# The sums of one weight pair on VectorE instead of GpSimd, traced one tile sooner: linear attention and a gated feed-forward layer

## The chip, the cores and the metric

The kernel runs on one core of one Trainium2 chip. The metric is device microseconds of one execution; of several runs the median counts. Beside the times there is one execution taken with the hardware profiler, whose trace is read below. In the text PE is TensorE, DVE is VectorE, ACT is ScalarE, POOL is GpSimd, SP is SyncE, as the profile writes them.

## The reference

Eight batches of eight heads, 576 positions, head size 64: linear attention (softmax of q over the head size, softmax of k over the positions, then q times the product of k and v). Its result, 4608 rows of 512, goes through a gated layer of width 1536.

```python
q_s = exp(q - max(q, -1)); q_s /= sum(q_s, -1) + 1e-9
k_s = exp(k - max(k, 2));  k_s /= sum(k_s, 2) + 1e-9
kv = einsum('bhsd,bhse->bhde', k_s, v)
x = einsum('bhsd,bhde->bhse', q_s, kv)      # then rows of B*S by H*D = 4608 x 512
out = ((x @ w_a) * (x @ w_b)) @ w_out       # 512 -> 1536 -> 512
```

The weights arrive as the bits of 64-bit floats and are turned into 32-bit floats on the chip.

## The kernel before

The 4608 rows are worked on in nine chunks of 512. The width 1536 is cut into twelve tiles f of 128, and two tiles make a pair i, six pairs in all. Each matmul of the large products is done three times, with a rounded high part and a remainder of each operand (`split`: ScalarE makes the high part at line 79, VectorE the remainder at line 82).

*The first chunk* is also the start of the kernel, in which everything is loaded and converted. For the tiles f = 2 to 11 one loop runs. In a round it loads weights two tiles ahead (`load_f`), converts the next tile's (`convert_ab`, `convert_wo`: ScalarE at line 103, VectorE at 107 and 113, GpSimd at 110), does a piece of the attention of the second and third chunk (`tasks`), multiplies the chunk with the tile's two weight halves (`gate_part`, line 510) into the banks k0 and k1, empties k0 by ScalarE (`gate_half`, `ga`, line 517), multiplies k1 onto it by VectorE (`gate_end`, line 521) and adds the product of the tile before with `w_out` to the output banks (`project_first`, line 545, `po`). The converted weights are stored to memory as `dy` (plain) and `dw` (split).

*From the second chunk on*, the product of a pair is done as a two by two block product with seven multiplications instead of eight (`product`, line 535: banks kx, ky, ka, kp). Four of the seven weight operands are sums of blocks: S1, S3, S2, S4. In the second chunk they are made pair by pair by `sums(i)`: four loads of `dy` into tiles `ws_y` (line 217, SyncE's queue), and four additions of 128x512 (line 225), on GpSimd, S1 first, then S3, S2 and S4, where S2 and S4 each read an earlier sum. `split_w` makes high part and remainder of each, and `put_w` stores it (line 204) for the later chunks, which load it again (`get_w`, line 208). The operands of the chunk itself (T1 to T4 and three blocks) come from `x_operands`: VectorE's differences at lines 484, 489 and 494, and splits into `xo`.

`sums(0)` is called in the last round, f = 11, and `sums(i + 1)` in the second chunk's pair i. So GpSimd makes the sums of the first pair (i = 0) and of the second one after the other. The first pair's four loads wait for room in the eight tiles of the name `wy`, which the conversion uses too.

Between the chunks stands a piece of attention for the third chunk: TensorE turns a maximum (pm, line 261), VectorE reduces it (line 263) and spreads it on a diagonal (line 265), TensorE adds that up (pmx, line 271), VectorE subtracts it (276), ScalarE takes the exponential (279), TensorE multiplies keys and values (pk, line 312), and VectorE scales the product (320 to 323, 81, 82). In the second chunk's pair i, VectorE adds ky to the copy u of kx (line 1098, made by ScalarE at 1097), ka to that (1100), then kp (1111), and so on.

*What sets the order.* The order of TensorE in the first chunk and that of the first tiles on the other engines is written out by hand (`in_order`). Elsewhere a scheduler places each engine's instructions when the program is built, from the order in which they are traced and from an estimate of the times; `issue_after(x)` keeps what is traced under it behind x. On the chip each engine then takes its instructions in that fixed order and waits on semaphores. The bank k0 holds the gates of the last tile before it holds kx of the second chunk's first pair, so kx waits for line 517.

Of the kernel before, what the change touches and what calls it, by code (L numbers as in the profile page):

```python
# [29 lines left out]
def linear_attention_then_gated_ffn(  # L30
# [18 lines left out]
    nc = tc.nc  # L49
# [4 lines left out]
    NF = 2 * NI  # L54
# [72 lines left out]
    def load_f(f):  # L127

        i, r = divmod(f, 2)
        for half in range(2):  # L130
            raw = sb.tile([P, DM], I64, name="raw", tag="xo", bufs=11)
            ins = nc.sync.dma_start(out=raw, in_=w_ab[i, r, half])
            raws[f, half] = raw
        raw = const.tile([P, DM], I64, name=f"wo{f}_raw", tag=f"wo{f}")
        with tc.issue_after(ins.ins):
            nc.sync.dma_start(out=raw, in_=w_out[f])
        raws[f, "o"] = raw
        return ins
# [20 lines left out]
    def convert_wo(f):  # L159
        y, parts = float_parts(raws.pop((f, "o")), wo_home(f))  # L160
        for part in parts:
            part()
        keep_wo(f, y)

    def split_wo(f):
        if f < 4:
            wo[f] = const.tile([P, 2, DM], F32R, name=f"wo{f}_w", tag=f"wo{f}")
        split(wo[f][:, 0], wo[f][:, 1], wo_first[f])
# [14 lines left out]
    def convert_ab(f, half):  # L183

        keep_ab(f, half, *whole_ab(f, half, to_float(raws.pop((f, half)))))
# [22 lines left out]
        nc.sync.dma_start(out=w.bitcast(F32), in_=dw[i, op].bitcast(F32))  # L208
        return w

    def sums(i):

        a = {}
        for r in range(2):
            for h in range(2):
                a[r, h] = sb.tile([P, DM], F32, name="ws_y", tag="wy", bufs=8)
                nc.sync.dma_start(out=a[r, h], in_=dy[i, r, h])
        sub, add = ALU.subtract, ALU.add
        for o, x, y, op in (
            ((1, 1), (1, 0), (1, 1), add),  # L220
            ((1, 0), (0, 0), (1, 0), sub),
            ((0, 0), (1, 1), (0, 0), sub),
            ((0, 1), (0, 1), (0, 0), sub),
        ):
            nc.gpsimd.tensor_tensor(out=a[o], in0=a[x], in1=a[y], op=op)
        return {S1: a[1, 1], S3: a[1, 0], S2: a[0, 0], S4: a[0, 1]}


# [247 lines left out]
    def x_operands(xf, which, box):  # L476

        b11, b12 = xf[:, 0:2, 0:H], xf[:, 0:2, H:T]
        b21, b22 = xf[:, 2:4, 0:H], xf[:, 2:4, H:T]
        for op in which:  # L480
            if op == T2:
                t1, t2 = t_tile(), t_tile()
                nc.vector.tensor_tensor(out=t1, in0=b12, in1=b11, op=ALU.subtract)
                nc.vector.tensor_tensor(out=t2, in0=b22, in1=t1, op=ALU.subtract)
                box["t1"], box["t2"] = t1, t2
                src = t2
            elif op == T3:
                src = t_tile()
                nc.vector.tensor_tensor(out=src, in0=b22, in1=b12, op=ALU.subtract)
            elif op == T1:  # L490
                src = box["t1"]
            elif op == T4:
                src = box["t2"]
                nc.vector.tensor_tensor(out=src, in0=b21, in1=src, op=ALU.subtract)
            else:
                src = {B11: b11, B21: b21, B22: b22}[op]
            o = xo_tile([P, 2, 2, H])
            split(o[:, 0], o[:, 1], src)
            box[op] = o


    def gate_banks(tags):
        return [ps.tile([P, T], F32, name=f"pt{n}", tag=tag) for n, tag in enumerate(tags)]

    def gate_part(f, x, n, pairs, pt):

        for g in pairs:
            w = blocks[f, g // 2][:, n, :, g % 2]
            for i, (wp, xp) in enumerate(((0, 0), (0, 1), (1, 0))):
                nc.tensor.matmul(  # L510
                    pt, w[:, wp], x[g][:, xp],
                    start=(g == 0 and i == 0), stop=(g == NP - 1 and i == 2),
                )

    def gate_half(f, pt):
        ga = sb.tile([P, T], F32, name="ga", tag=f"gh{f % 2}", bufs=1)
        nc.scalar.copy(out=ga, in_=pt)  # L517
        return ga

    def gate_end(ga, pt):  # L520
        return nc.vector.tensor_tensor(out=ga, in0=pt, in1=ga, op=ALU.mult)
# [21 lines left out]
    def project_first(f, g, po):  # L543
        for t in range(TT):
            nc.tensor.matmul(  # L545
                po[t], g[:, t * P:(t + 1) * P], wo_first[f],
                start=(f == 0), stop=(f == NF - 1),
            )
# [257 lines left out]
    at = {}  # L806
# [179 lines left out]
    sy = {}  # L986
# [21 lines left out]
    for f in range(2, NF):  # L1008
        if 1 < f - 1 < NF - 3:
            tasks[f - 1][0]()  # L1010
        if f + 2 < NF:
            load_f(f + 2)

        with tc.issue_after(at["end", f - 2].ins):
            convert_wo(f)
            if f + 1 < NF:
                convert_ab(f + 1, 0)
                convert_ab(f + 1, 1)


        n = f - 3
        if n < 0:
            copies = ()
        else:
            copies = tasks[n][2]()
        if n + 1 < NF - 3:
            with tc.issue_after(startup[0]), tc.issue_after(at["end", max(f - 2, 1)].ins):
                tasks[n + 1][1]()
        if f == NF - 1:
            with tc.issue_after(at["end", f - 1].ins):  # L1030
                split_wo(0)
                split_wo(1)
            sy[0] = sums(0)
            x_operands(xfs[1], early + late, xo)
        if f > 2:
            pts = gate_banks(("k0", "k1"))
            for h in range(2):
                gate_part(f, x0, h, range(NP), pts[h])
                if h == 0:
                    with ExitStack() as pinned:  # L1040
                        for copy in copies or ():
                            pinned.enter_context(tc.issue_after(copy.ins))
                        at["ga", f] = gate_half(f, pts[0])
            at["end", f] = gate_end(at["ga", f], pts[1])
        if n >= 0:
            tasks[n][3]()
        project_first(*pending, po)
        pending = (f, at["ga", f])
    in_order((E.PE,), by_hand, len(traced))
# [15 lines left out]
    for c in range(1, NCH):  # L1065
# [3 lines left out]
        x, xo = xo, {}  # L1069
        for i in range(NI):  # L1070
# [19 lines left out]
            if c == 1:  # L1090
                if i + 1 < NI:
                    sy[i + 1] = sums(i + 1)
                    split_wo(2 * i + 2)
                    split_wo(2 * i + 3)
# [8 lines left out]
            end = c == NCH - 1 and i == NI - 1  # L1103
# [78 lines left out]
```

## Time and profile before

| | |
|---|---|
| median of 3 runs | 975.72 us (975.56 to 975.88) |
| the profiled execution | 974.85 us |
| its span in the trace | 972.8 us |
| granted clock of TensorE, mean | 0.995 |
| TensorE busy | 942.0 us, 97% of the span |
| VectorE busy | 632.7 us, 65% |
| ScalarE busy | 393.0 us, 40% |
| GpSimd busy | 108.1 us, 11% |

Busy time of TensorE is modelled at its end, so 97% is no measure of how well it is used; it says that it hardly waits. The first 186 us hold the first chunk and the beginning of the second; the shares of the table are means over stages that differ, so the waits and the order of time are read below, and not the shares.

### The profile page before, as it was taken

What the parts mean: (1) busy time and instruction counts of PE and PEld (TensorE: products, weight loads), DVE (VectorE), ACT (ScalarE), POOL (GpSimd) and SP (SyncE); (2) the same over time, 40 slices, a digit from 0 to 9 for tenths busy, and PEclk for the clock granted to TensorE, in tenths of its full rate; (3) what the DMA queues carried; (4) which work ended last, traced back from release to release, by engine and by line L of the source; (5) the groups of instructions that cost most, each with busy time, mean ns of one, the idle gap of its engine ahead of it and who ended that gap; (6) DMA issues with size and microseconds to landing.
All of it is one profiled execution on the core that took longest, in us unless ns stands there. A gap on an engine that the chain in (4) does not pass through costs nothing.

```text
span 972.8 us, 16975 instructions
## 1 busy us (share of the span) xinstructions
PE 942.0 (97%) x6159; PEld 843.8 (87%) x6159; DVE 632.7 (65%) x1245; ACT 393.0 (40%) x1085; POOL 108.1 (11%) x92
## 2 busy tenths in 40 slices
PE   4989998999999999999999999999999999999998
PEld 3656765899999999999998999999999999999997
DVE  7986878987686747665665657565766446653433
ACT  7777754553372416332443235223623263221101
POOL 1544443522000000000000000000000000000000
PEclk9999998999999999999999999999999999999999
DMA  9999585989999968897788779877998687767761
GB/s 353 412 382 361 207 292 190 405 290 340 311 346 279 366 237 264 308 375 254 263 307 330 283 250 344 305 282 259 338 295 281 233 315 249 293 224 276 254 209 58
DMA packets 97586, 282.60 MB, mean 290 GB/s; under 512 B 11680, under 2 KB 12256, under 8 KB 97504
## 3 DMA queue, kind: packets, MB, share of 16 engines
q1 hardware_dynamic: 97504, 281.52, 81.1%
q8 instruction: 49, 0.80, 0.3%
q14 instruction: 33, 0.27, 0.1%
HBM read 241.40 MB, written 37.98 MB: 287 GB/s over the span
## 4 chain that ended last, share of the span: by engine, by line
PE 82%; DVE 7%; DMA 4%; issue 3%; ACT 2%; SPq 1%; POOL 1%; DVEq 0%; POOLq 0%; ACTq 0%
PE po L556 27%; PE kp L535 14%; PE ka L535 13%; PE kx L535 13%; PE ky L535 7%; PE pk L312 3%; PE px L466 2%; DMA ws<-dw 1%; DVE wy L113 1%; DMA dy<-wy 1%; PE po L545 1%; PE pt L510 1%; POOL wr L110 1%; DMA raw<-in_w_ab 1%; ACT wy L103 1%
## 5 line engine op out<-in xcount | busy, mean ns | idle before, releaser
L556 PE MATMUL po<-wo_w,gh 128*128 128x512 f32 x768 | 230.8, 396 | 0.0
L535 PE MATMUL kx<-xo,ws 128*128 128x256 f32 x1152 | 163.9, 284 | 3.2 <-ACT ga L517 3.2
L556 PEld LDWEIGHTS po<-wo_w,gh 128*128 128x128 f32 x768 | 138.7, 189 | 26.3 <-ACT gh L79 0.3
L535 PE MATMUL ka<-xo,ws 128*128 128x256 f32 x1152 | 161.3, 283 | 0.0
L535 PE MATMUL kp<-xo,ws 128*128 128x256 f32 x1152 | 156.7, 283 | 1.4 <-DVE u L1098 1.4
L535 PEld LDWEIGHTS kx<-xo,ws 128*128 128x128 f32 x1152 | 150.2, 189 | 6.1 <-ACT ga L517 3.6
L535 PEld LDWEIGHTS ka<-xo,ws 128*128 128x128 f32 x1152 | 149.9, 189 | 3.9 <-issue 0.5
L535 PEld LDWEIGHTS kp<-xo,ws 128*128 128x128 f32 x1152 | 146.8, 189 | 3.9 <-issue 1.6
L556 PE MATMUL po<-wo_w,gl 128*128 128x512 f32 x384 | 140.2, 396 | 0.0
L79 ACT CAST gh<-cc 128x512 fp32r<-128x512 f32 x96 | 57.6, 621 | 131.3 <-DVE cc L1122 124.5
L1121 DVE TENSOR_TENSOR cc<-kp,u 128x512 f32<-128x512 f32 x48 | 33.2, 691 | 103.7 <-PE kp L535 103.7
L1112 ACT COPY cc<-kx 128x256 f32<-128x256 f32 x48 | 17.9, 372 | 185.8 <-PE kx L535 185.8
L556 PEld LDWEIGHTS po<-wo_w,gl 128*128 128x128 f32 x384 | 71.6, 188 | 16.3 <-DVE gl L82 0.4
L380 ACT ACTIVATE qt<-qt,st 128x64 f32<-128x64 f32 x224 | 74.9, 338 | 25.2 <-DVE st L377 18.3
L1111 DVE TENSOR_TENSOR cc<-kp,u 128x512 f32<-128x512 f32 x48 | 32.9, 686 | 71.7 <-PE kp L535 71.5
L535 PE MATMUL ky<-xo,ws 128*128 128x256 f32 x576 | 77.8, 284 | 1.1 <-DMA ws<-dw 1.1
L535 PEld LDWEIGHTS ky<-xo,ws 128*128 128x128 f32 x576 | 72.1, 189 | 1.9 <-DVE xf L658 1.2
L510 PE MATMUL pt<-xo,ws 128*128 128x512 f32 x288 | 71.8, 406 | 1.1 <-DVE ws L925 1.1
L82 DVE TENSOR_TENSOR gl<-cc,gh 128x512 fp32r<-128x512 f32 x96 | 66.5, 700 | 8.1 <-ACT gh L79 8.1
L510 PEld LDWEIGHTS pt<-xo,ws 128*128 128x128 f32 x288 | 54.7, 193 | 14.3 <-DVE ws L925 1.5
L244 POOL PARTITION_ALL_REDUCE mx<-m x20 | 14.4, 722 | 460.8 <-DVE m L255 429.6
L1097 ACT COPY u<-kx 128x512 f32<-128x512 f32 x48 | 28.0, 583 | 81.1 <-PE kx L535 81.0
(144 smaller groups left out, 1202.6 us busy)
## 6 DMA issues: line engine op xcount, KB each, us to landing
ws<-dw SPq DMA_DIRECT2D x312, 512.0 KB, 5.3
dw<-ws SPq DMA_DIRECT2D x42, 512.0 KB, 6.8
mr<-dq SPq DMA_DIRECT2D x112, 128.0 KB, 4.2
raw<-in_w_ab SPq DMA_DIRECT2D x24, 512.0 KB, 7.7
out<-ot SPq DMA_DIRECT2D x36, 256.0 KB, 4.4
vt<-in_v SPq DMA_DIRECT2D x28, 325.0 KB, 7.7
qt<-in_q SPq DMA_DIRECT2D x32, 256.0 KB, 5.6
kt<-in_k SPq DMA_DIRECT2D x24, 320.0 KB, 5.5
```

The costliest lines, as they stand in the source:

```text
L79: nc.scalar.copy(out=hi, in_=src)
L82: return nc.vector.tensor_tensor(out=lo, in0=src, in1=hi.bitcast(F32), op=ALU.subtract)
L312: nc.tensor.matmul(pk, kt[:, j].rearrange("p h d -> p (h d)"), vt[:, j], start=(j == 0), stop=(j == J - 1),)
L380: nc.scalar.activation(out=qt[:, j, h], in_=qt[:, j, h], func=AF.Exp, bias=st[:, h, 0, j:j + 1], accum_out=st[:, h, 1, j:j + 1],)
L466: nc.tensor.matmul(px[:, s], w, m[:, s], start=(i == 0), stop=(i == 2))
L510: nc.tensor.matmul(pt, w[:, wp], x[g][:, xp], start=(g == 0 and i == 0), stop=(g == NP - 1 and i == 2),)
L535: ins = nc.tensor.matmul(pt[:, n], w[:, n, wp, c], x[:, xp, c], start=(first and n == 0 and i == 0), stop=(i == 5), skip_group_check=True,)
L556: ins = nc.tensor.matmul(po[t], a[:, ts], wo[f][:, w], start=(f == 0 and i == 0), stop=(f == NF - 1 and i == 2),)
L1097: nc.scalar.copy(out=u2, in_=kx)
L1111: nc.vector.tensor_tensor(out=cc[:, 3], in0=kp, in1=u3, op=ALU.add)
L1112: nc.scalar.copy(out=cc[:, 0, 0], in_=kx[:, 0])
L1121: nc.vector.tensor_tensor(out=cc[:, 1], in0=kp, in1=u2, op=ALU.add)
```

## The change

`sums` gets an engine as an argument. The call for the first pair moves from the last round, f = 11, to the end of the round before, f = 10, behind that round's gates and attention piece in the order of tracing, and its four additions go to VectorE. Its loads may start behind the end of tile 8's gates. The five other calls stay as they were, on GpSimd.

```diff
-    def sums(i):
+    def sums(i, engine=nc.gpsimd):
...
-            nc.gpsimd.tensor_tensor(out=a[o], in0=a[x], in1=a[y], op=op)
+            engine.tensor_tensor(out=a[o], in0=a[x], in1=a[y], op=op)
...
                 split_wo(0)
                 split_wo(1)
-            sy[0] = sums(0)
             x_operands(xfs[1], early + late, xo)
...
         if n >= 0:
             tasks[n][3]()
+        if f == NF - 2:
+            with tc.issue_after(at["end", f - 2].ins):
+                sy[0] = sums(0, nc.vector)
         project_first(*pending, po)
```

The lines behind move by two in the new kernel: line 1098 becomes 1100, 1111 becomes 1113.

The scheduler's order moves with it. Below are VectorE's instructions between the chunks, before the change, behind lines 484 and 489:

```order
L82 TENSOR_TENSOR xo<-xt,xo 128x512 x2
L494 TENSOR_TENSOR xt<-xf,xt 128x512
L82 TENSOR_TENSOR xo<-xt,xo 128x512
L82 TENSOR_TENSOR wo_w<-wo_w 128x512
L263 TENSOR_REDUCE mc<-pm 128x1
L82 TENSOR_TENSOR xo<-xf,xo 128x512 x2
L82 TENSOR_TENSOR xo<-xt,xo 128x512
L265 TENSOR_SCALAR m_1363<-ident,mc 128x128
```

The same stretch of VectorE after the change:

```order
L225 TENSOR_TENSOR ws_y<-ws_y 128x512
L82 TENSOR_TENSOR xo<-xt,xo 128x512
L225 TENSOR_TENSOR ws_y<-ws_y 128x512
L82 TENSOR_TENSOR xo<-xt,xo 128x512 x2
L494 TENSOR_TENSOR xt<-xf,xt 128x512
L82 TENSOR_TENSOR wo_w<-wo_w 128x512
L263 TENSOR_REDUCE mc<-pm 128x1
L82 TENSOR_TENSOR xo<-xf,xo 128x512
L225 TENSOR_TENSOR ws_y<-ws_y 128x512
L82 TENSOR_TENSOR xo<-xf,xo 128x512
L82 TENSOR_TENSOR xo<-xt,xo 128x512
L265 TENSOR_SCALAR m_1375<-ident,mc 128x128
```

Three sums (S1, S3, S2) stand among the operands ahead of line 265, S4 stands right behind it, and one split of `xo` has moved ahead of line 494.

TensorE at the same place, the difference from before (-) to after (+): the last gates, then the first products of the second chunk, where the second kx row is the pair's other product into that bank:

```order
 L535 MATMUL kx<-xo,ws 128x256 x12
-L271 MATMUL pmx<-m_1363,ones 128x128
+L271 MATMUL pmx<-m_1375,ones 128x128
 L545 MATMUL po_492<-wo_w,ga 128x512
 L545 MATMUL po_493<-wo_w,ga 128x512
 L545 MATMUL po_494<-wo_w,ga 128x512
 L545 MATMUL po_495<-wo_w,ga 128x512
-L535 MATMUL ky<-xo,ws 128x256 x12
+L535 MATMUL kx<-xo,ws 128x256 x11
+L535 MATMUL ky<-xo,ws 128x256 x12
+L535 MATMUL ka<-xo,ws 128x256 x12
 L545 MATMUL po_492<-wo_w,ga 128x512
```

Eleven of the twelve matmuls of that other product, which stood behind pk, now stand ahead of ky; ka stands ahead of the last tile's po.

VectorE some 20 us later, ahead of the sum u of the second pair (line 1098, `u_1666`), before the change:

```order
L82 TENSOR_TENSOR kvl_1697<-wholes,kvh_1696 128x128
L385 RECIPROCAL st<-st 128x2x4
L255 TENSOR_TENSOR m_1686<-m_1686,kt 128x128
L384 TENSOR_SCALAR st<-st 128x2x4
L263 TENSOR_REDUCE mc<-pm 128x1
L385 RECIPROCAL st<-st 128x2x4
L265 TENSOR_SCALAR m_1694<-ident,mc 128x128
L1098 TENSOR_TENSOR u_1666<-ky,u_1666 128x512
```

The same place of VectorE after the change:

```order
L82 TENSOR_TENSOR ws<-ws_y,ws 128x2x256
L254 TENSOR_TENSOR m_1686<-m_1685 128x128
L82 TENSOR_TENSOR kvl_1697<-wholes,kvh_1696 128x128
L385 RECIPROCAL st<-st 128x2x4
L82 TENSOR_TENSOR gl_1659<-cc,gh_1658 128x512
L1100 TENSOR_TENSOR u_1666<-ky,u_1666 128x512
L255 TENSOR_TENSOR m_1686<-m_1686,kt 128x128
```

Five small operations of the attention that stood ahead of u stand behind it, and a split of a third-pair sum has come ahead of it.

## Rows read from the trace of the kernel before

**Rows 1.** Waits of TensorE up to 200 us: total, times, longest (us).

```profile
PE kx L535 <- ACT ga L517: 3.2, 1, 3.2
...
PE kp L535 <- DVE u L1098: 1.4, 1, 1.4
```

**Rows 2.** Waits of TensorE from 200 us to the end.

```profile
PE ky L535 <- DMA ws<-dw: 1.1, 1, 1.1
```

**Rows 3.** Timeline of TensorE: start, length (us), instruction, in brackets the idle time before.

```profile
25.44 0.63 PE L883 MATMUL pq<-ident,qts 128*128 128x128 f32 x4 [2.50 <-issue]
...
69.83 0.30 PE L299 MATMUL pkb<-ident,kt 128*128 128x128 f32 x1 [2.07 <-DVE wholes L323]
...
155.48 2.02 PE L535 MATMUL kx<-xo,ws 128*128 128x256 f32 x12 [3.20 <-ACT ga L517]
158.24 0.80 PE L271 MATMUL pmx<-m,ones 128*128 128x128 f32 x2 [0.75 <-DVE m L265]
...
170.86 1.28 PE L312 MATMUL pk<-vt,kt 128*128 128x130 f32 x10
...
173.42 1.60 PE L535 MATMUL kx<-xo,ws 128*128 128x256 f32 x12
174.86 1.60 PE L535 MATMUL ka<-xo,ws 128*128 128x256 f32 x12
...
182.82 0.33 PE L261 MATMUL pm<-ident,m 128*128 128x128 f32 x1 [0.46 <-DVE m L255]
184.55 1.66 PE L535 MATMUL kp<-xo,ws 128*128 128x256 f32 x12 [1.40 <-DVE u L1098]
```

**Rows 4.** Stretches: length, TensorE busy, granted clock, DMA share, GB/s.

```profile
71.00:71.50 0.50, 0.50 (x4) 0.79 1.02 410
74.50:75.00 0.50, 0.50 (x3) 0.80 1.06 411
156.50:157.00 0.50, 0.50 (x5) 0.62 0.00 0
163.00:163.50 0.50, 0.50 (x2) 0.55 0.98 401
```

**Rows 5.** Timeline of VectorE between the chunks.

```profile
142.28 0.69 DVE L521 TENSOR_TENSOR ga<-pt,ga 128x512 f32<-128x512 f32 x1 [3.04 <-PE pt L510]
...
143.49 1.76 DVE L82 TENSOR_TENSOR wo_w<-yo,wo_w 128x512 fp32r<-128x512 f32 x1
...
151.96 1.75 DVE L494 TENSOR_TENSOR xt<-xf,xt 128x512 f32<-128x512 f32 x1
...
155.31 0.68 DVE L82 TENSOR_TENSOR wo_w<-wo_w 128x512 fp32r<-128x512 f32 x1
...
157.92 0.27 DVE L265 TENSOR_SCALAR m<-ident,mc 128x128 f32<-128x128 f32 x1
```

**Rows 6.** Timeline of GpSimd, 135 to 200 us.

```profile
141.58 13.26 POOL L225 TENSOR_TENSOR ws_y<-ws_y 128x512 f32<-128x512 f32 x8 [3.66 <-DMA ws_y<-dy]
171.49 5.65 POOL L225 TENSOR_TENSOR ws_y<-ws_y 128x512 f32<-128x512 f32 x4 [16.66 <-DMA ws_y<-dy]
```

**Rows 7.** Timeline of ScalarE: the copy that empties k0.

```profile
154.84 0.58 ACT L517 COPY ga<-pt 128x512 f32<-128x512 f32 x1
```

**Rows 8.** Timeline of SyncE's queue: the loads of the second pair's sums.

```profile
139.82 3.78 SPq L217 DMA_DIRECT2D ws_y<-dy  x4
```

**Rows 9.** Timeline of VectorE from pk's end to u of the second pair.

```profile
172.18 0.16 DVE L320 TENSOR_SCALAR den<-pk 128x1 f32<-128x1 f32 x1 [0.42 <-PE pk L312]
...
173.22 1.26 DVE L82 TENSOR_TENSOR kvl<-kv,kvh 128x128 fp32r<-128x128 f32 x1
...
182.21 0.29 DVE L82 TENSOR_TENSOR kvl<-wholes,kvh 128x128 fp32r<-128x128 f32 x1
...
182.53 0.24 DVE L255 TENSOR_TENSOR m<-m,kt 128x128 f32<-128x128 f32 x1
...
183.72 0.68 DVE L1098 TENSOR_TENSOR u<-ky,u 128x512 f32<-128x512 f32 x1
```

## The prediction

> **What bounds the kernel now.** The first view to read is the list of waits of TensorE. Up to 200 us it holds a dozen of them; from 200 us to the end there is one, of 1.1 us [rows 1, 2]. Behind 186 us TensorE therefore runs as one unbroken stream, of the same matmuls in both kernels, and what the end of the first chunk wins or loses arrives at the end undiminished. The change acts between 142 and 186 us. So the question is when TensorE starts kp of the second pair, at 184.55 before [rows 3]: everything behind it follows without a wait.
>
> The second view is TensorE's timeline there, with what ended each idle stretch. After the last gates (155.48 − 3.20 = 152.28) it idles 3.20 us for the bank k0, which ScalarE's copy ga has to empty, runs kx, idles again until pmx at 158.24, works on to 182.4, and idles 0.46 and 1.40 us around pm until kp. The first two waits are 3.95 us together. From about 156.6 to 163.4 the granted clock is at its lower level, 1.2 GHz [rows 4].
>
> The third view, VectorE's timeline, says why. From 142.28 to 157.92 it has hardly any idle time, but its operations on 128x512 with both inputs in SBUF take 1.75 us each at 143.49 and 151.96, and 0.68 us at 155.31; one out of PSUM takes 0.69 at 142.28 [rows 5]. Over the slow part GpSimd makes eight sums, 141.58 to 154.84: the first pair's four and the second pair's four [rows 6]. Between 143.49 and 155.31 stand seven VectorE operations, 1.69 us from one to the next; each pays 1.75 − 0.68 = 1.07 us, 7.5 us in all. ScalarE's ga copy at 154.84 [rows 7] stands behind a copy that needs VectorE's L494 (done at 153.71), and pmx needs VectorE's L265 (157.92). So VectorE, held up by GpSimd, is what ends last.
>
> **The change part by part.**
>
> *Four sums leave GpSimd and come to VectorE.* Three of them (S1, S3, S2) stand ahead of L265, one behind. An operation of this shape that nothing holds up takes a pitch of 0.60 us: 155.31 to 157.92 holds four such and one small reduction of 0.2 [rows 5]. Price 3 x 0.60 = 1.8 us. GpSimd keeps the second pair's four. They can't start before their loads, the last of which is issued by 143.60 [rows 8] and was there when GpSimd's fifth sum began (half of 13.26 us behind 141.58: 148.2). I take 147.5. So all four still fall on VectorE's busy stretch: 4 x 1.07 = 4.3 us in place of 7.5. L265 comes 7.5 − 4.3 − 1.8 = **1.4 us sooner**, at 156.5, and pmx at 156.8. Bounds: 2.5, if one sum meets an operation out of PSUM; 0.3, if a fifth operation is held up.
>
> [...]
>
> *The bank k0.* From 142.28 to the end of L494 VectorE has eleven slots of 0.60, so 148.9, and up to 153.2 with GpSimd's sums in between. Two ScalarE copies of about 0.6 follow, and kx starts between 152.3 and 154.4 instead of 155.48. Alone that wins nothing, because pmx stands behind kx: the idle time moves from before kx to behind it, 156.8 − 152.28 − 1.44 (kx, twelve matmuls at the pitch of 173.42 to 174.86) = 3.1 us in place of 3.95.
>
> *The clock.* After 3.1 us of idle I expect TensorE at 1.2 GHz again; the nearest row is the wait of 3.20. Behind that the lower level held 6.8 us, with 0.75 us of idle inside it; behind the wait of 2.07 at 69.83 it held 3.4 (71.3 to 74.7), with none [rows 3, 4]. Here pmx, po and the hoisted kx matmuls follow each other, so I take 3.4. The loss was (6.8 − 0.75)/2 = 3.0 and is now 3.4/2 = 1.7: **1.3 us won**. Bounds 0 and 3.0.
>
> *Eleven kx matmuls are hoisted* from behind pk to before it, 11 x 0.12 = 1.3 us. They are the same work, but VectorE's run that begins when pk is done (172.18) and ends with u of the second pair (183.72) starts later by them. pk ends 1.4 + 1.3 − 1.3 = 1.4 us sooner.
>
> *VectorE's run from pk to u* is 11.54 us with next to no idle time, and kp waits for it [rows 3, 9]. In the new order five small operations (from L255 at 182.53 to u, 1.19 us) no longer stand before u, and one split of 0.60 does: **0.6 us won**. GpSimd's sums of the third pair lie over the run (from 171.49, 5.65 us); a kvl takes 1.26 us there and 0.29 outside [rows 6, 9]. Their loads come sooner by about as much as pk does, so I leave that; bounds ± 0.9.
>
> *What costs nothing.* The first pair's loads had landed by 141.58, when GpSimd's first sum began [rows 6]; VectorE needs them at 145. SyncE's queue then stands, in both orders, behind the first split of a sum on VectorE, which moves with L265. If a load came 4 us late, VectorE would stand in front of L494, and the 3.20 us would be back.
>
> The sum: kp starts 1.4 + 0.6 = 2.0 us sooner. I take 1.8, leaving 0.2 for small waits in a new order of some 180 rows on TensorE. The profiled execution took 974.85 us with a span of 972.8; the median of the runs is 975.72, and the difference is taken from it: **973.9 us**.
>
> **The rivals.**
>
> *A second low stretch of the clock.* TensorE reaches kp of the second pair 1.4 + 1.3 = 2.7 us sooner, but VectorE is ready only 2.0 sooner, and pm (0.3) now stands behind kp: the idle time there grows from 1.86 to 2.9 us, about 2.3 in one piece (before ka the rest). For a fall of the clock: waits of 2.07 and 3.20 us were followed by one. Against: 2.50 us before 25.44 was not, nor were 0.46 and 1.40 [rows 3]. Price 3.4/2 = 1.7: 975.6 us.
>
> [...]
>
> *No low stretch at all.* If 3.1 us of idle leaves the clock alone as the 2.50 did, 1.7 more is won: 972.2. If one sum of GpSimd also meets nothing: 971.1.
>
> *Two long low stretches.* While the clock is low TensorE waits again, at 158 for ScalarE's copy of kx, which now stands behind the copy of VectorE's fourth sum, and at 185 for VectorE. Then each low stretch lasts 6.8 us like the one before: the 1.3 isn't won, and the second costs 3.0. 973.9 + 4.3 = 978.2 us, slower than before. It is decided by whether VectorE is later than TensorE again within the low stretch. For it: that is what happened at 158.24. Against: 3.6 us of matmuls po stand ready this time.
>
> *The run from pk to u takes it all.* If GpSimd's third-pair sums hold up two more of VectorE's operations, 1.07 each, kp starts where it did: 975.7.
>
> **How the numbers follow.** About 0.2% (2 us) is what a measurement of this kernel can tell from no change. Forecast 0.40 (972.9 to 974.8; 0.16 of it beyond 0.2%), second low stretch 0.22, no low stretch 0.22, two long ones 0.12, the run takes it all 0.04. Faster 0.16 + 0.22 = 0.38, slower 0.12, the same 0.50. The range goes from 971.2 (no low stretch and a sum fewer) to 976.9 (a second low stretch and the first as long as before).
>
> **What would show it.** In the profile of the changed kernel: four VectorE operations of 1.75 us instead of seven, from 146 to 148 on; kx of the first pair by 154.4; pmx at 156.5 to 157.1, then the lower clock for 3.4 us; pk's end near 170.8; an idle stretch of 2 to 2.5 us before kp, which starts near 182.7; granted clock 1.00 from 183 to 190. It would be wrong with pmx later than 158, with a granted clock of 0.50 behind 183, or with a wait of TensorE behind 190.

## The result and the profile after

The changed kernel takes 978.26 us (median of 20 runs, 973.57 to 981.52) beside 975.62 us for the kernel before (20 runs, 971.56 to 977.50). The ratio is 1.0029 with a 95% interval of 1.0019 to 1.0039: slower by 2.8 us, 1.9 to 3.8. The profiled execution of the changed kernel took 977.2 us, with a span of 975.4.

First the waits of TensorE, up to 200 us and then behind it (total, times, longest).

```profile
PE pmx L271 <- DVE m L265: 2.9, 1, 2.9
...
PE kp L535 <- DVE u L1100: 1.8, 1, 1.8
```

```profile
PE ky L535 <- ACT xo L79: 2.2, 1, 2.2
PE po L556 <- ACT gh L79: 0.5, 2, 0.3
PE ka L535 <- ACT xo L79: 0.2, 1, 0.2
```

Up to 200 us the list is what the change aimed at: the 3.2 us of kx are gone, pmx has 2.9 in place of 0.75 [rows 1, 3]. Behind 200 us there are waits that the kernel before doesn't have, the longest of them ky's for xo, and its 1.1 us wait for a DMA [rows 2] is gone.

**Around the change**, TensorE's timeline:

```profile
152.73 1.58 PE L535 MATMUL kx<-xo,ws 128*128 128x256 f32 x12
157.24 0.49 PE L271 MATMUL pmx<-m,ones 128*128 128x128 f32 x2 [2.93 <-DVE m L265]
157.57 3.60 PE L545 MATMUL po<-wo_w,ga 128*128 128x512 f32 x8
160.60 1.87 PE L535 MATMUL kx<-xo,ws 128*128 128x256 f32 x11
...
168.59 1.28 PE L312 MATMUL pk<-vt,kt 128*128 128x130 f32 x10
...
181.44 1.81 PE L535 MATMUL kp<-xo,ws 128*128 128x256 f32 x12 [1.77 <-DVE u L1100]
...
183.11 3.55 PE L556 MATMUL po<-wo_w,gh 128*128 128x512 f32 x8
```

kp of the second pair starts at 181.44 instead of 184.55 [rows 3]: 3.1 us won. VectorE, GpSimd and ScalarE there:

```profile
148.93 0.68 DVE L494 TENSOR_TENSOR xt<-xf,xt 128x512 f32<-128x512 f32 x1
149.53 0.68 DVE L82 TENSOR_TENSOR wo_w<-wo_w 128x512 fp32r<-128x512 f32 x1
150.13 0.28 DVE L263 TENSOR_REDUCE mc<-pm 128x1 f32<-128x128 f32 x1
150.33 1.59 DVE L82 TENSOR_TENSOR xo<-xf,xo 128x512 fp32r<-128x512 f32 x1
151.84 1.79 DVE L225 TENSOR_TENSOR ws_y<-ws_y 128x512 f32<-128x512 f32 x1
153.55 1.77 DVE L82 TENSOR_TENSOR xo<-xf,xo 128x512 fp32r<-128x512 f32 x1
155.25 1.74 DVE L82 TENSOR_TENSOR xo<-xt,xo 128x512 fp32r<-128x512 f32 x1
156.91 0.28 DVE L265 TENSOR_SCALAR m<-ident,mc 128x128 f32<-128x128 f32 x1
```

```profile
147.71 8.73 POOL L225 TENSOR_TENSOR ws_y<-ws_y 128x512 f32<-128x512 f32 x4 [8.12 <-DMA ws_y<-dy]
```

```profile
150.17 0.58 ACT L517 COPY ga<-pt 128x512 f32<-128x512 f32 x1
```

Four operations of VectorE are held up, not seven, all beside the second pair's sums on GpSimd; ga comes 4.7 us sooner than in [rows 7]; L265 at 156.91 instead of 157.92 [rows 5].

The granted clock in stretches (length, then busy time of TensorE, its weight loads, VectorE, ScalarE and GpSimd, the granted clock, the DMA's share and GB/s):

```profile
157.00:160.00 3.00, 2.76 (x8) 1.48 (x9) 3.00 (x6) 1.62 (x3) 0.00 (x0) 1.00 0.26 108
...
182.00:184.00 2.00, 2.00 (x13) 1.90 (x12) 2.00 (x7) 1.18 (x4) 0.00 (x0) 0.71 0.99 388
184.00:186.00 2.00, 2.00 (x6) 1.52 (x6) 2.00 (x8) 0.00 (x0) 0.00 (x0) 0.50 1.05 412
...
275.00:278.00 3.00, 2.95 (x14) 2.95 (x15) 3.00 (x6) 2.08 (x4) 0.00 (x0) 0.50 0.67 248
```

Behind the 2.93 us of idle the granted clock stays at 1.00; behind the 1.77 us before kp it falls to 0.50, and eight output products take 3.55 us where the same eight took 2.02 in the kernel before, at 186.05 and a granted 1.00. (The views give the clock as a share of full speed. No run shows it in GHz; what the prediction and the expectation of e6 call 1.2 GHz is the share 0.50, as in every us from 157 to 163 of the kernel before.) That gives 1.7 of the 3.1 us back, so the lead behind 190 us is 1.4.

**At the boundary of the second chunk and the third**, about 80 us behind the stretch in which the change was to act, TensorE's timeline of the kernel before and then of the changed one:

```profile
264.95 0.22 PE L466 MATMUL px<-qh,kvh 128*128 128x128 f32 x1
...
265.77 0.22 PE L466 MATMUL px<-ql,kvh 128*128 128x128 f32 x1
...
271.99 1.10 PE L556 MATMUL po<-wo_w,gl 128*128 128x512 f32 x4
...
273.16 1.46 PE L535 MATMUL ky<-xo,ws 128*128 128x256 f32 x11
```

```profile
270.34 1.10 PE L556 MATMUL po<-wo_w,gl 128*128 128x512 f32 x4
271.27 0.22 PE L466 MATMUL px<-qh,kvh 128*128 128x128 f32 x1
...
274.45 0.39 PE L535 MATMUL ky<-xo,ws 128*128 128x256 f32 x1 [2.16 <-ACT xo L79]
275.05 0.58 PE L535 MATMUL ka<-xo,ws 128*128 128x256 f32 x1 [0.22 <-ACT xo L79]
275.43 2.55 PE L535 MATMUL ky<-xo,ws 128*128 128x256 f32 x11
```

px is the attention product of the fourth head pair of the third chunk, six small matmuls. From it VectorE makes xf and xt, ScalarE xo, and xo is what ky and ka of the third chunk multiply. Before, px stands among kx, 7 us ahead of the last output product; after, it stands behind that product, at 271.27. So nothing of TensorE's own is left to cover the chain behind it. On VectorE and ScalarE after:

```profile
267.75 0.69 DVE L82 TENSOR_TENSOR ql<-qtt,qh 128x512 fp32r<-128x512 f32 x1 [0.49 <-ACT qh L79]
272.33 0.69 DVE L658 TENSOR_TENSOR xf<-px,mr 128x512 f32<-128x512 f32 x1 [3.89 <-PE px L466]
273.05 0.69 DVE L484 TENSOR_TENSOR xt<-xf,xt 128x512 f32<-128x512 f32 x1
```

```profile
273.78 1.74 ACT L79 CAST xo<-xt 128x512 fp32r<-128x512 f32 x3 [0.95 <-DVE xt L484]
```

px's last operand, ql, is there at 268.44; px runs 2.8 us later only because of its place in TensorE's order. Counted on the same work (the end of px and the last output product, then the end of ka), the changed kernel is 0.8 us ahead in front of the boundary (272.29 against 273.09) and 3.6 behind after it (279.54 against 275.93): **4.4 us lost**, of which 2.16 + 0.22 are waits and 1.7 the lower clock behind them (0.50 from 275 to 278). At the end 1.1 us of it is back, since the kernel before waits that long for a DMA [rows 2] and the changed one doesn't.

Added up: 3.1 us won at kp, 1.7 lost to the clock behind it, 0.6 between 190 and 270 us (0.32 of that a wait of po for gh at 265.58, the rest not traced further), 4.4 lost at the boundary and 1.1 back make 2.5 us lost; the two spans differ by 2.6 (975.4 against 972.8).

### The profile page after: what moved, and what is told of

It reads as the page before. It is cut to its first block, busy times and chain, and to the rows that moved or that the text cites. A ratio compares the mean times of both kernels' runs of the same rounds, so it can differ in the third digit from the quotient of the medians.

```text
span 975.4 us, 16962 instructions
## 1 busy us (share of the span) xinstructions
PE 943.9 (97%) x6159; PEld 846.5 (87%) x6159; DVE 627.5 (64%) x1249; ACT 392.4 (40%) x1085; POOL 102.1 (10%) x88
## 4 chain that ended last, share of the span: by engine, by line
PE 86%; DVE 3%; DMA 1%; ACT 1%; issue 0%; POOL 0%; SPq 0%; ACTq 0%; POOLq 0%; DVEq 0%
PE po L556 28%; PE kp L535 14%; PE ka L535 14%; PE kx L535 13%; PE ky L535 7%; PE pt L510 3%; PE pk L312 3%; PE px L466 2%; PE po L545 2%; DMA qt<-in_q 1%; DVE xo L82 1%; DMA out<-ot 0%; DVE st L377 0%; DVE ws_y L225 0%; DVE wy L113 0%
```

## The experiments

Theory 1: the gain around the change is real, and the loss is px's new place, which the program's scheduler chose when the sums changed engine. Theory 2: the sums on VectorE, with the low clock at 183 us, are the loss. Theory 3: it is the sums' earlier place. All ratios are against runs of the kernel before on the same chip, with 95% intervals.

**e6_fault_in_before**: the kernel before with px put last.

```
+        if c == 1 and f == NF - 1:
+            for px in late_px:
+                tc.add_manual_dep(
+                    px, project_last[0].ins.name,
+                    mybir.DependencyInfo(mybir.DependencyClass.NoSync, mybir.DependencyReason.DATA),
...
```

> The kernel before (sums of the first pair on GpSimd, at the old place), with one pin: the six matmuls that make px of the fourth head pair for the third chunk may be issued only behind the last output product (po) of the second chunk. In the kernel before they stand among kx at 265-266.5 us; in the changed kernel they stand at 271.3. The order of TensorE is that of the kernel before up to the pin. Theory 1 (the changed kernel loses its time at this place, because px comes last there): ky and ka of the third chunk wait for xo about 2.2 + 0.2 us and the granted clock then falls to 1.2 GHz for 3 to 4 us (1.7 us more), so the kernel is 3 to 4.4 us slower than before (978.6 to 980), with the wait ky<-ACT xo of 2 us or more in its list of waits. Theory 2 (the time goes to VectorE's sums themselves and to the second stretch at the lower clock at 183-187 us): no sum is on VectorE here, so the time is within 1 us of the kernel before.

1.0056 (1.0040 to 1.0072), slower by 3.9 to 7.0 us. In its profile the wait is there to the hundredth:

```profile
274.38 0.22 PE L466 MATMUL px<-qh,kvh 128*128 128x128 f32 x1
...
277.56 0.38 PE L537 MATMUL ky<-xo,ws 128*128 128x256 f32 x1 [2.16 <-ACT xo L79]
278.16 0.38 PE L537 MATMUL ka<-xo,ws 128*128 128x256 f32 x1 [0.22 <-ACT xo L79]
278.38 1.47 PE L537 MATMUL ky<-xo,ws 128*128 128x256 f32 x11
```

The fault alone makes the kernel before slow, so theory 2 isn't needed for the loss. In this execution no low clock came behind the wait (eleven ky in 1.47 us, as in the 1.46 of the kernel before at a granted 1.00, and not in 2.55 as in the changed kernel at 0.50), so the boundary cost 2.9 us there by the same count (the two waits and 0.5 of smaller gaps), and the run was some 2 us late already before it (ScalarE's copy of kx of the third pair at 202.87, before 200.30), by nothing that the edit touches: up to the pin TensorE's order is that of the kernel before. So the 5.5 us of the ratio are more than the 4.4 that theory 1 names, and its interval reaches down to them; where the rest comes from is not shown.

**e3_px_between**: the changed kernel with px put back, between the last two tiles' output products.

```
+        if c == 1 and f == NF - 1:
+            with tc.issue_after(lastpx[2, 3].ins):
+                project(f, ghl, po)
```

> The changed kernel with one pin: the last output products of the second chunk (those of the last tile, four banks) may be issued only behind px of the fourth head pair of the third chunk, which so moves from 271.3 us to about 268.5, between the output products of the last tile but one and those of the last. TensorE's order is otherwise that of the changed kernel up to there. Theory 1 (px last is the loss): px's inputs stand at about 268.5 in the changed kernel, so px runs there with no wait or one under 0.5 us, xf, xt and xo are made while 3.2 us of output products run, the 2.2 + 0.2 us wait of ky and ka goes, and with it the low clock behind it: 3.5 to 4.4 us are won against the changed kernel, 974 to 975 us, 0.5 to 1.5 us under the kernel before. Theory 2 (VectorE's sums and the low clock at 183-187 us are the loss): the time stays with the changed kernel, 977 to 979 us.

0.9982 (0.9968 to 0.9995): 974.79 us, 4.6 us of ratio below the changed kernel. Its TensorE timeline:

```profile
267.77 0.22 PE L466 MATMUL px<-qh,kvh 128*128 128x128 f32 x1
...
272.10 1.57 PE L536 MATMUL ky<-xo,ws 128*128 128x256 f32 x11 [0.34 <-DVE xo L82]
```

px runs without a wait, and 0.34 is left of the 2.4 us. Theory 1 holds from both sides: put in, the fault costs; taken out, the change is a small gain. Theory 2 falls with it: this kernel has the sums on VectorE and a low clock from 182.2 to 185.6 us, and is no slower than the kernel before. A rival is that both pins also change TensorE's order in places behind 289 us. The traces speak against it: from the end of ka at the boundary to the end of the span the kernel before takes 696.9 us, the changed one 695.9, e6 697.6 and e3 695.5.

**e1_engine_only and e2_place_only**: the two halves of the change (sums takes its engine as an argument in both).

```
-            sy[0] = sums(0)
+            sy[0] = sums(0, nc.vector)
```

> One half of the change alone: the first pair's sums go to VectorE, but are traced where they were, in front of the first kx of the second chunk. TensorE's order then again has px of the fourth head pair behind the last output product of the second chunk. Theory 1 (px last is the loss, and the engine's change brings it about): about as slow as the changed kernel or somewhat slower, 977.5 to 980, with the wait of ky for xo near 272-275 us. Theory 3 (the loss comes from the earlier place, its loads and its trace order): within 1 us of the kernel before.

1.0009 (0.9997 to 1.0020), 977.25 us, with the 2.2 us wait of ky for xo in the list: px stands last here too. The time is a little under what theory 1 gave, and by the ratios 2.0 us under the changed kernel. In the trace no low clock follows the wait at the boundary (ScalarE idles 2.43 us there for the next kx, 3.92 in the changed kernel), so that it costs 2.9 us here, as in e6.

```
+        if f == NF - 2:
+            with tc.issue_after(at["end", f - 2].ins):
+                sy[0] = sums(0)
```

> The other half alone: the first pair's sums are traced one tile sooner, but stay on GpSimd. TensorE's order is that of the kernel before in every row; a few loads on SyncE's queue and casts on VectorE change places between 130 and 180 us. Theory 1: px keeps its place among kx at 265 us, so no wait for xo at the third chunk, and the time is within 1 us of the kernel before (974.6 to 976.6). Theory 3 (the earlier place is the loss): 977.5 to 979.

0.9966 (0.9955 to 0.9978), 972.46 us: better than every theory said. px keeps its place, so it is the engine's change that moves it; but the earlier place, which the prediction priced at nothing, is worth 2.1 to 4.4 us by itself (e7 below, in which the sums run in the same way, gives 1.0 to 3.3). GpSimd's timeline shows what is different:

```profile
139.01 6.00 POOL L225 TENSOR_TENSOR ws_y<-ws_y 128x512 f32<-128x512 f32 x4
149.37 6.79 POOL L225 TENSOR_TENSOR ws_y<-ws_y 128x512 f32<-128x512 f32 x4 [4.36 <-DVE xo L82]
```

The first pair's sums are done at 145.0 and hold up one operation of VectorE at full length (143.81, 1.75 us). Then VectorE runs undisturbed until the second pair's sums hold up four, as in the changed kernel, but without the three sums of 0.60 on VectorE. m starts at 156.64 instead of 157.92 [rows 5], and the low clock lasts from 156.8 to 160.2 instead of from about 156.6 to 163.4; kp of the second pair comes 2.1 us sooner, at 182.44. What is left in both kernels is the second pair's overlap.

**e7, e8, e9: the second pair's sums held back, first try.** Theory A says that the overlap of GpSimd's sums with VectorE's operations holds m up and with it TensorE; theory B that another wait ends last behind it, so that the overlap costs nothing. A pin put these sums behind L265, the operation that makes m:

```
+                if behind is not None:
+                    pinned.enter_context(tc.issue_after(behind.ins))
                 engine.tensor_tensor(out=a[o], in0=a[x], in1=a[y], op=op)
```

> The first pair's sums one tile sooner on GpSimd (the half of the change that ran as e2_place_only, 972.46 us), and the second pair's sums on GpSimd held back: each may be issued only behind the VectorE operation that makes the first m (the diagonal of key maxima that pmx waits for). TensorE's order is the same in every row. In e2_place_only the second pair's sums run from 149.37 to 156.2 us and four VectorE operations in that time take 1.6 to 1.8 us instead of 0.68; m starts at 156.64 and pmx has waited 3.1 us for it. Theory A (what holds m up is the overlap of GpSimd's sums with VectorE's operations, 4 x 1.07 us): m starts at about 152.5, the 3.1 us wait of pmx goes, some of it comes back where the held-back sums now overlap the splits behind m: 1 to 3 us under e2_place_only, 969.5 to 971.5. Theory B (another wait ends last behind it, so the overlap is no cost): within 0.7 us of e2_place_only.

> The changed kernel with px of the fourth head pair pinned between the last output products (as in e3_px_between, 974.79 us), and the second pair's sums, which stay on GpSimd, held back behind the VectorE operation that makes the first m. TensorE's order is that of e3_px_between in every row. There the second pair's sums start at 146.31 us, four VectorE operations take 1.6 to 1.8 us, m starts at 156.21 and pmx has waited 2.93 us for it. Theory A (the overlap is what holds m up): m at about 152, the wait of pmx is gone or under 0.5 us, 1 to 3 us under e3_px_between (972 to 973.8). Theory B: within 0.7 us of e3_px_between.

> The kernel before with nothing of the change in it: the first pair's sums on GpSimd at the old place; only the second pair's sums are held back behind the VectorE operation that makes the first m. TensorE's order is that of the kernel before in every row. Theory A (the overlap of GpSimd's sums with VectorE's operations is the cost of this stretch, whatever pair they belong to): GpSimd's run of eight sums, 141.6 to 154.8 us, is cut to four that end near 148; three to four VectorE operations behind that take 0.68 instead of 1.75 us, m starts 3 to 4 us sooner than its 157.9, and kx and pmx, which waited 3.2 and 0.75 us, wait 1.5 to 3.5 us less in all: 972 to 974.5 us. Theory B (the change's gain came from the place or the engine of the first pair's sums alone): within 0.7 us of the kernel before.

0.9978 (0.9966 to 0.9990), 0.9992 (0.9979 to 1.0004) and 0.9996 (0.9982 to 1.0010): nothing won, and nothing tested. In e3 and e6 such pins held, between instructions of one engine. Here the sums stand on GpSimd and L265 on VectorE, and the pin made no wait between them on the chip; the second pair's sums ran where they had run (in e7 from 150.63, with m at 157.60). Theory B isn't shown by this, since the cause had not been taken away. e7 then stands as a second measurement of e2.

**e10, e11, e12: held back in fact.** The second pair's first sum now waits on a semaphore for L265.

```
+            ins = nc.gpsimd.tensor_tensor(out=a[o], in0=a[x], in1=a[y], op=op)
+            if behind is not None:
+                tc.add_manual_dep(
+                    ins.ins, behind.ins.name,
+                    mybir.DependencyInfo(mybir.DependencyClass.Sync, mybir.DependencyReason.DATA),
...
+                behind = None
```

> As e7_place_late_second, but the second pair's first sum now waits in fact (on a semaphore) for the VectorE operation that makes the first m; in e7_place_late_second the pin set only an order, and the sums ran from 150.63 to 157.1 us as before. First pair's sums one tile sooner on GpSimd; TensorE's order that of the kernel before in every row. Theory A (the overlap of the second pair's sums with VectorE holds m up, 4 operations x 1.07 us): GpSimd is idle from 146 us to m, xo and ws take 0.68 us each, m starts at about 153.3 instead of 157.60, the 3.1 us wait of pmx shrinks to under 0.5 us; the sums behind m then overlap the splits beside TensorE's output products: 1.5 to 3 us under e2_place_only and e7_place_late_second (972.5 and 973.7), 970 to 972. Theory B (something else ends last behind it): m sooner by the same 4 us, but the time within 0.7 us of those two.

> The changed kernel with px of the fourth head pair pinned between the last output products (e3_px_between, 974.79 us), and the second pair's first sum waits on a semaphore for the VectorE operation that makes the first m. TensorE's order is that of e3_px_between in every row. Theory A: no GpSimd sum runs beside VectorE before m, its four operations there take 0.68 us instead of 1.6 to 1.8, m starts near 152 instead of 156.21, and the wait of pmx (2.93 us) goes: 1.5 to 3 us under e3_px_between, 972 to 973.5. Theory B: within 0.7 us of e3_px_between.

> The kernel before with nothing of the change in it, except that the second pair's first sum waits on a semaphore for the VectorE operation that makes the first m. (In e9_late_second_only the pin set only an order, and the eight sums ran from 140.6 to 153.4 us in one go.) TensorE's order is that of the kernel before in every row. Theory A (every GpSimd sum beside VectorE ahead of m costs about 1.07 us, whatever pair it belongs to): four sums from 140.6 to about 147, then none; of the seven VectorE operations of 1.75 us three are left, m starts about 4 us sooner than 157.9, kx (3.2 us) and pmx (0.75) wait 3 to 4 us less in all; 972 to 973.5 us, the gain that the change aimed at, with no sum moved to VectorE. Theory B: within 0.7 us of the kernel before.

e10: 0.9945 (0.9926 to 0.9963), 970.04 us. e11: 0.9947 (0.9928 to 0.9966), 969.86. e12: **0.9935 (0.9914 to 0.9955), 969.61 us**, 6.3 us under the kernel before. e12 has nothing of the change in it. Its GpSimd, its VectorE, TensorE's waits from 140 to 200 us, its kp of the second pair, and the clock (columns as above):

```profile
142.59 6.32 POOL L227 TENSOR_TENSOR ws_y<-ws_y 128x512 f32<-128x512 f32 x4 [4.45 <-DMA qt<-in_q]
154.92 7.27 POOL L227 TENSOR_TENSOR ws_y<-ws_y 128x512 f32<-128x512 f32 x4 [6.01 <-DVE m L274]
```

```profile
147.67 1.78 DVE L498 TENSOR_TENSOR xt<-xf 128x512 f32<-128x512 f32 x1
...
150.75 0.68 DVE L503 TENSOR_TENSOR xt<-xf,xt 128x512 f32<-128x512 f32 x1
...
154.57 0.27 DVE L274 TENSOR_SCALAR m<-ident,mc 128x128 f32<-128x128 f32 x1
```

```profile
PE kp L544 <- DVE u L1107: 1.4, 1, 1.4
PE kx L544 <- ACT ga L526: 0.8, 1, 0.8
PE pm L270 <- DVE m L264: 0.5, 1, 0.5
```

```profile
178.70 1.66 PE L544 MATMUL kp<-xo,ws 128*128 128x256 f32 x12 [1.40 <-DVE u L1107]
```

```profile
150.00:180.00 30.00, 27.39 (x171) 22.07 (x170) 26.89 (x57) 19.97 (x60) 12.94 (x8) 1.00 0.86 309
```

As soon as GpSimd stands still, VectorE's operations fall from 1.78 to 0.68 us; m comes at 154.57 instead of 157.92, and of kx's 3.2 and pmx's 0.75 us [rows 3] 0.8 is left. Theory A is shown, with the prediction's own price of 1.07 us: the operations held up fall from seven to three and a part. But the waits are only 3.2 of e12's 6.3 us. The clock is the other half: the granted clock stays at 1.00 from 150 to 180 us in all four kernels with the hold (e10 to e13), and the low stretch that it leaves out had cost the kernel before 3.0 us, as the prediction works it out; kp of the second pair is at 178.70 instead of 184.55 [rows 3]. Theory A had counted the waits alone, so e12 came out under its range of 972 to 973.5. e11 did too, e10 lies in its own. Between e10, e11 and e12 the intervals overlap: once the second pair is held back, it can't be measured where the first pair's sums are made.

**e13_after_hold_second**: the hold in the changed kernel, px left last. It is the fourth corner of px last or between, sums held or not.

> The changed kernel with its px of the fourth head pair left where it is (behind the last output product of the second chunk), and the second pair's first sum waits on a semaphore for the VectorE operation that makes the first m. TensorE's order is that of the changed kernel in every row. With e3_px_between, e11_px_between_hold_second and the changed kernel this is the fourth of four: px behind or between, sums held or not. Theory 1 (px last costs 4 to 4.5 us whatever goes before it) and theory A (the hold wins what it won in e11, about 5 us): m starts near 154 without a wait of pmx, the wait of ky for xo is there again (2.2 us, at some 267 to 270 us), and the time is that of e11 (969.9 us) plus 3.5 to 4.5, 973.4 to 974.4 us. Rival (the wait at the chunk's boundary comes from something that the late sums delay): the wait of ky for xo is gone or under 0.5 us, and the time is within 1 us of e11.

0.9995 (0.9983 to 1.0008), 974.32 us; the 2.16 us wait of ky for xo is there. The profiled execution was the slowest of the twelve (978.80 us).

| ratio to the kernel before | px last | px between | difference |
|---|---|---|---|
| sums not held | 1.0029 (the change) | 0.9982 (e3) | 0.0047, 4.6 us |
| sums held | 0.9995 (e13) | 0.9947 (e11) | 0.0048, 4.7 us |
| difference | 0.0034, 3.3 us | 0.0035, 3.4 us | |

The two effects add up, as far as this can tell: by the intervals of the ratios each difference is known to some 1.6 to 2.3 us. px's place costs about 4.6 us with the hold and without it, and the overlap that the change leaves in place costs another 3.3.

## Why the prediction was wrong

**The step that failed** is the premise of the sum: that everything behind kp of the second pair "follows without a wait", so that the win of the first chunk arrives undiminished. It was read from the waits of the kernel before [rows 2], which hold for the order of the kernel before. But the changed kernel has an order of its own, some 180 rows of TensorE different, and some of them lie far behind the change. I put "small waits in a new order" at 0.2 us, and didn't look for what stands last ahead of each chunk's boundary. The step's term, for which the sum had 0.2 at most, was 4.4 us in the profile, 4.6 by the ratios. e6 and e3 show that it is this. Two of the signs of being wrong that the prediction names came true: a wait of TensorE behind 190, and a granted clock of 0.50 behind 183.

**What held.** L265 1.4 us sooner: the trace has 1.0, and the last gates end 0.45 later than before (152.73 against 152.28), so 1.4 by the stretch's own measure. Four held-up operations for seven, at 1.07: four, at 0.9 to 1.1. kx without its wait, idle time of 2.9 in place of 3.95 (forecast 3.1): so. Eleven hoisted kx, 1.3 us: they stand at 160.60. The run from pk to u, 0.6 won: pk is 2.27 us sooner and kp 3.1, so 0.8.

**What was mis-sized.** The clock: 1.3 us was forecast and 3.0 won, since no low stretch came at 157 us. That, with the rest, is why kp was 3.1 us sooner and not 1.8. The rival of a low stretch before kp came true beside it: 1.7 us, as priced. With those two the sum up to 190 us is 1.4 us won, against 1.8; had the boundary cost nothing, the time would have lain near e3's 974.8, inside the range. That 1.4 comes so near to 1.8 is luck: two misses on the clock, 1.7 us each, stand against each other. It is luck too that the rival of two long low stretches gives 978.2: no stretch of 6.8 us came, and the loss lies at the boundary. (The low end of the range is given as 971.2; its own sum gives 971.1.)

**What a held-up operation cost, and when the clock fell.** A held-up operation of VectorE lost 0.9 to 1.1 us in the changed kernel (1.59 to 1.79 us in place of 0.68), and in e12 about 1.1 came back for each (0.68 in place of 1.78). Of the twenty sums left on GpSimd in the changed kernel the shortest took 1.27 us, the median 1.32, so what an operation lost was a little less than a whole sum. And it goes both ways: the first of the four sums at 147.71 took 3.67 us, while VectorE's operations behind each other took 0.68; only behind the small reduction at 150.13 was one of them held up. By what rule the two engines take turns, the runs don't show.

The clock fell at 182.9, behind 1.77 us of idle in one piece and 0.40 and 0.20 ahead of it, and not behind 2.93; in e11, with 1.8, 0.6 and 0.2 us in the same place, it didn't fall (ScalarE idles 7.69 us for the next kx there, 9.24 in the changed kernel). So neither the length of the last gap nor the sum of the pieces, 2.4 us in the one and 2.6 in the other, tells it in these runs.

**What stays open.** Why the scheduler puts px last once the sums are on VectorE wasn't tried beyond the two halves: e1 does it and e2 doesn't. Nor is it settled when the clock falls (below), and with it 1.7 to 3 us for a low stretch in any single run of this kernel.

## What to carry to other kernels

Where a scheduler makes the order, a change of one instruction's engine can move others far away: compare the orders to the end, and above all what stands last ahead of each boundary where the next stage's operands are made. And before moving work off an engine that disturbs another, ask whether it is needed yet: here a wait of the second pair's sums, wanted some 20 us later, won 6.3 us (half of it by the clock) where moving the first pair's lost 2.8. An ordering pin that made no wait on the chip didn't hold another engine back (e7: the sums ran from 150.63, m came at 157.60); look at the trace that the cause is really gone before reading the time.

## What the runs showed of the hardware

The granted clock did not follow the length of an idle stretch. Behind 2.93 us before pmx it stayed at 1.00 in the changed kernel and in e3_px_between; behind 3.14 in e2 it fell to 0.50 from 157 to 160 us, and so behind 2.5 in e1. Behind the same 2.16 us at the boundary it stayed in e6 and e1 and fell to 0.50 in the changed kernel, for 3.5 us, and in e13, for 7 (the slowest of its runs). And the 1.4 us before kp were followed by a fall in e10 (180 to 184 us) but not in e12.

In the changed kernel a 128x512 sum on GpSimd and an operation of VectorE with both inputs in SBUF held each other up, in either direction: 1.6 to 1.8 us for the operation instead of 0.68, and 3.67 us for a sum that began under a run of such operations, where the shortest took 1.27.
